# Gate and up products with their last 64 rows paired in the array's rows, column chunks in pairs, a written order on every engine, and the normalization on Pool

## The chip, the cores and the metric

The kernel runs on one core of a Trainium2 chip. The metric is device time in microseconds (us), the median over runs. A core has five engines that run at the same time and wait for each other through semaphores: TensorE (PE; its weight loads are listed as PEld), VectorE (DVE), ScalarE (ACT), GpSimd (Pool) and SyncE (SP), which here only issues transfers. Transfers run on 16 DMA engines; SP and Pool each have a queue into them. SBUF is the working memory of 128 partitions, PSUM the memory into which TensorE accumulates; here it is used as eight banks of 128 x 512 float32.

## The reference, cut to what matters

```python
x  = A_x                                  # [1, 2048, 576]
xn = _layernorm(x)                        # mean and variance over 576, eps 1e-5
s  = attention(xn, wq, k_cache, v_cache, wo)     # 32 heads, head width 128
gate = xn @ w_gate                        # [2048, 4608]
up   = xn @ w_up                          # [2048, 4608]
h    = sigmoid(gate) * up
g    = silu(h @ w_down)                   # [2048, 576]
out  = x + s * g
# returned: out and its gradients for x, k_cache, v_cache, wq, wo, w_gate, w_up, w_down
```

The first stage computes layernorm and the two products with `w_gate` and `w_up` (Wg, Wu). For the backward pass it keeps, beside `h`, the two factors `a = sigmoid(gate)` and `b = h * (1 - a)`.

## The kernel before, in words

The 2048 rows of x are 16 tiles of 128 rows (`st`). The width 576 is four slices of 128 and a last one of 64 (`dts`, `DT` = 5). The width 4608 is nine column chunks of 512 (`FCH`, `NFC`).

**Stage 1** (lines 164 to 263) is all that the change rewrites.

- *Loads.* SP loads two x tiles (L183), then chunk 0 of Wg and Wu, slice by slice (L194, L195), then the other 14 x tiles (L197), then chunks 1 and 2, then 3 to 5 and 6 to 8. The last slice has 64 rows; the other 64 partitions of `wg_sb`, `wu_sb` and `xnT` are set to zero by Pool (`zpad`, L160), so that every product runs over 128 rows.
- *Normalization*, `ln_tile` (from L207): statistics on DVE (L211, L213), square root on ACT (L215), reciprocal and bias on DVE (L216, L219), the scaling on ACT (L220). Then `transpose_to` turns the tile with five TensorE transposes (L59) and copies them to `xnT` on DVE (L42) and ACT (L40).
- *Products.* Three groups of three chunks; within a group all 16 row tiles; within a tile the three chunks. Each chunk takes five products into `g_ps` (L249) and five into `u_ps` (L252), 128 x 128 by 128 x 512, one PSUM bank each. Tiles are normalized two ahead during the first group.
- *After the products*, per chunk: two sigmoids on ACT (L253 gives `a`, L255 gives 1 - a as `oma`), `h` and `b` on DVE (L256, L257). Per tile and group Pool issues one store each to the arrays `h_d`, `a_d`, `b_d` (L259, L262, L263), 384 KB each.
- Pool also issues the store of the normalized x (L235) and the load of Wd (L236).
- The order on every engine is chosen by the scheduler of the language from priorities and dependencies.

**Stage 2** (from L265) reads `h` back transposed (`hT`, two loads issued in stage 1 at L261 and the others by `load_hT` at L282; the first two lie in the room that x had, the others in the room of the weights), multiplies by Wd (L306: per row tile 36 steps of one 512-wide and one 64-wide product) and forms the gradients of the silu.

**The rest**: 32 attention heads forward and backward in an order written out by hand on TensorE, DVE and ACT, then the output product, the gradients of the weights (which read `a`, `b`, `h` in `load_abh`; L806 and L812 are the gradient of Wg and Wu, L779 the product that precedes it) and the gradient of x. In L812 the last 64 columns of x are multiplied twice into the two halves of the output partitions, so two half-width products stand side by side in the array's columns.

Of the kernel before, what the change touches and what calls it, by code (L numbers as in the profile page):

```python
# [9 lines left out]
bf = mybir.dt.bfloat16  # L10
f32 = mybir.dt.float32
# [84 lines left out]
def kernel(  # L96
# [42 lines left out]
    a_d = dram.tile([S, F], bf, name="a_d")  # L139
    b_d = dram.tile([S, F], bf, name="b_d")  # L140
    h_d = dram.tile([S, F], bf, name="h_d")
# [9 lines left out]
    eps_t = pers.tile([P, 1], f32, name="eps_t")  # L151
    nc.vector.memset(eps_t[:], EPS)

    alt = Alt(nc)
    KPAD = dts[-1][1] < P
    d_last, kd_last = dts[-1]

    def zpad(t):
        if KPAD:
            nc.gpsimd.memset(t[kd_last:, DT - 1, :], 0.0)  # L160

    def kfull(i, kd):
        return P if KPAD else kd

    FCH = min(512, F)
    NFC = F // FCH
    GRP = ldiv(NFC, 3)
# [6 lines left out]
    zpad(xnT)  # L174
    dsT = pk.tile([P, DL, S], bf, name="dsT")
    wo_h = pk.tile([P, D], bf, name="wo_h")
    with tc.tile_pool(name="pa", bufs=1) as pa:
        wd_sb = pa.tile([P, FT, D], bf, name="wd_sb")
        with tc.tile_pool(name="a1w", bufs=1) as wp:
            a0x = tc.alloc_tile_pool(name="a0x", bufs=1, side="right")  # L180
            x_all = a0x.tile([P, NT, D], bf, name="x_all")
            XF = min(2, NT)
            nc.sync.dma_start(x_all[:, 0:XF, :], x2[0:XF * P, :].rearrange("(t p) d -> p t d", p=P))  # L183
            xn_st = x_all
            wg_sb = wp.tile([P, DT, F], bf, name="wg_sb")
            wu_sb = wp.tile([P, DT, F], bf, name="wu_sb")
            zpad(wg_sb)
            zpad(wu_sb)
            WSPL = GRP * FCH
            bounds = [0, FCH] + list(range(WSPL, F + 1, WSPL)) if WSPL > FCH else list(range(0, F + 1, WSPL))  # L190
            for bi in range(len(bounds) - 1):
                c0, c1 = bounds[bi], bounds[bi + 1]
                for i, (d0, kd) in enumerate(dts):
                    nc.sync.dma_start(wg_sb[:kd, i, c0:c1], B_w_gate[d0:d0 + kd, c0:c1])  # L194
                    nc.sync.dma_start(wu_sb[:kd, i, c0:c1], B_w_up[d0:d0 + kd, c0:c1])  # L195
                if bi == 0 and NT > XF:
                    nc.sync.dma_start(x_all[:, XF:, :], x2[XF * P:, :].rearrange("(t p) d -> p t d", p=P))  # L197
            FMAX = nc.vector.BN_STATS_FMAX
            nchunk = 1
            while D % nchunk != 0 or D // nchunk > FMAX:  # L200
                nchunk += 1
            with tc.tile_pool(name="a0", bufs=3) as sb0, tc.tile_pool(name="a0ps", bufs=2, space=PSUM) as ps0, \
                    tc.tile_pool(name="a1r", bufs=2) as rows, tc.tile_pool(name="a1t", bufs=3) as tmpp, \
                    tc.tile_pool(name="a1ps", bufs=3, space=PSUM) as ps:

                def ln_tile(st):
                    xt = x_all[:, st, :]  # L207
                    stats = sb0.tile([P, nchunk, nc.vector.BN_STATS_DIM], f32, name="stats")
                    xr = xt.rearrange("p (c f) -> p c f", c=nchunk)
                    for c in range(nchunk):  # L210
                        nc.vector.bn_stats(stats[:, c, :], xr[:, c, :])  # L211
                    mv = sb0.tile([P, nc.vector.BN_AGGR_DIM], f32, name="mv")
                    nc.vector.bn_aggr(mv[:], stats[:])  # L213
                    std = sb0.tile([P, 1], f32, name="std")
                    nc.scalar.activation(std[:], mv[:, 1:2], AF.Sqrt, bias=eps_t[:], scale=1.0)  # L215
                    nc.vector.reciprocal(rstd_all[:, st:st + 1], std[:])  # L216
                    xn_t = xn_st[:, st, :]
                    nbias = sb0.tile([P, 1], f32, name="nbias")
                    nc.vector.scalar_tensor_tensor(nbias[:], mv[:, 0:1], -1.0, rstd_all[:, st:st + 1], op0=ALU.mult, op1=ALU.mult)  # L219
                    nc.scalar.activation(xn_t, xt, AF.Identity, bias=nbias[:], scale=rstd_all[:, st:st + 1])  # L220
                    transpose_to(nc, ps0, xn_t, D, xnT, st * P, ident, alt)

                LA = 2
                for st in range(min(LA, NT)):
                    ln_tile(st)
                for grp in range(NFC // GRP):
                    if grp == 1:
# [3 lines left out]
                    for st in range(NT):  # L231
                        if grp == 0 and st + LA < NT:
                            ln_tile(st + LA)
                        if grp == 0 and st == NT - 1:
                            nc.gpsimd.dma_start(xn_d[:, :].rearrange("(t p) d -> p t d", p=P), xn_st[:])  # L235
                            nc.gpsimd.dma_start(wd_sb[:], B_w_down.rearrange("(t p) d -> p t d", p=P))  # L236
                        srows = slice(st * P, (st + 1) * P)
                        a_row = rows.tile([P, GRP * FCH], bf, name="a_row")
                        b_row = rows.tile([P, GRP * FCH], bf, name="b_row")
                        h_row = rows.tile([P, GRP * FCH], bf, name="h_row")  # L240
                        for c in range(GRP):
                            fc = grp * GRP + c
                            fs = slice(fc * FCH, (fc + 1) * FCH)
                            cs = slice(c * FCH, (c + 1) * FCH)
                            g_ps = ps.tile([P, FCH], f32, name="g_ps")
                            u_ps = ps.tile([P, FCH], f32, name="u_ps")
                            for i, (d0, kd) in enumerate(dts):
                                kk = kfull(i, kd)
                                nc.tensor.matmul(g_ps[:], lhsT=xnT[:kk, i, srows], rhs=wg_sb[:kk, i, fs], start=(i == 0), stop=(i == DT - 1))  # L249
                            for i, (d0, kd) in enumerate(dts):  # L250
                                kk = kfull(i, kd)
                                nc.tensor.matmul(u_ps[:], lhsT=xnT[:kk, i, srows], rhs=wu_sb[:kk, i, fs], start=(i == 0), stop=(i == DT - 1))  # L252
                            nc.scalar.activation(a_row[:, cs], g_ps[:], AF.Sigmoid)  # L253
                            oma = tmpp.tile([P, FCH], bf, name="oma")
                            nc.scalar.activation(oma[:], g_ps[:], AF.Sigmoid, scale=-1.0)  # L255
                            nc.vector.tensor_tensor(h_row[:, cs], u_ps[:], a_row[:, cs], op=ALU.mult)  # L256
                            nc.vector.tensor_tensor(b_row[:, cs], h_row[:, cs], oma[:], op=ALU.mult)  # L257
# [724 lines left out]
```

## Time and profile before

| | us |
|---|---|
| three runs | 5168.2, 5173.1, 5188.1 |
| median | 5173.1 |
| the profiled execution | 5171.4 |
| its span, first to last instruction | 5169.6 |
| mean granted clock of TensorE | 0.994 of full speed |
| first product of stage 1 | 8.24 |
| first product of stage 2 | 350.0 |
| first product of the attention stage (L424) | about 500 |

Times in the profile are counted from the span's start. A group line gives the source line, the engine, the operation, what it writes and reads, the shape, the count, then busy time and the mean of one in ns, then the idle time of the engine just before it and what ended that. A chain of waits is followed back from the last instruction, at each step to what released it.

### The profile page before, as it was taken

What the parts mean: (1) busy time and instruction counts of PE and PEld (TensorE: products, weight loads), DVE (VectorE), ACT (ScalarE), POOL (GpSimd) and SP (SyncE); (2) the same over time, 40 slices, a digit from 0 to 9 for tenths busy, and PEclk for the clock granted to TensorE, in tenths of its full rate; (3) what the DMA queues carried; (4) which work ended last, traced back from release to release, by engine and by line L of the source; (5) the groups of instructions that cost most, each with busy time, mean ns of one, the idle gap of its engine ahead of it and who ended that gap; (6) DMA issues with size and microseconds to landing.
All of it is one profiled execution on the core that took longest, in us unless ns stands there. A gap on an engine that the chain in (4) does not pass through costs nothing.

```text
span 5169.6 us, 125543 instructions
## 1 busy us (share of the span) xinstructions
PE 5042.8 (98%) x54160; PEld 3506.0 (68%) x54160; DVE 3245.6 (63%) x5063; ACT 2288.2 (44%) x2886; POOL 1389.8 (27%) x1978
## 2 busy tenths in 40 slices
PE   8999999999999999999999999999989999999999
PEld 3444777777777777777777777777755666554554
DVE  5545888888888888888888888888733222210111
ACT  6531665565566555655655665566501222100000
POOL 2222332233233323332332333233222222111000
PEclk9999999999999999999999999999999999999999
DMA  7486999999999999999999999999998776697775
GB/s 280 183 215 162 194 193 200 190 195 198 193 197 194 193 191 197 199 199 196 200 194 196 199 193 200 199 198 198 207 223 230 203 202 191 194 249 164 159 152 119
DMA packets 2710366, 1013.31 MB, mean 196 GB/s; under 512 B 2523312, under 2 KB 2643888, under 8 KB 2709808
## 3 DMA queue, kind: packets, MB, share of 16 engines
q1 hardware_dynamic: 2628256, 726.57, 81.3%
q0 software_dynamic: 81552, 278.70, 18.0%
q8 instruction: 423, 6.93, 0.5%
q14 instruction: 135, 1.11, 0.1%
HBM read 172.54 MB, written 201.00 MB: 72 GB/s over the span
## 4 chain that ended last, share of the span: by engine, by line
PE 85%; DVE 6%; DMA 5%; issue 3%; ACT 0%; SPq 0%; POOL 0%; DVEq 0%; ACTq 0%; POOLq 0%
PE acckv L544 15%; PE acc L525 14%; PE acc L923 8%; PE dp L495 8%; PE sp L465 6%; PE accw L806 5%; DVE sneg L467 5%; PE accp L424 4%; PE dh L779 3%; PE g_ps L249 3%; PE u_ps L252 3%; PE acc L306 3%; PE accd L793 3%; DMA dST<-dSq 3%; PE acc L861 2%
## 5 line engine op out<-in xcount | busy, mean ns | idle before, releaser
L476 ACT ACTIVATE Pq<-sneg,nm 128x2048 bf16<-128x2048 bf16 x512 | 1024.5, 2001 | 389.5 <-DVE sneg L467 386.4
L525 PE MATMUL acc<-Kn,dST 128*128 128x128 bf16 x8192 | 1065.2, 219 | 34.6 <-DMA dST<-dSq 34.0
L525 PE MATMUL acc<-Vn,PT 128*128 128x128 bf16 x8192 | 1025.2, 219 | 10.5 <-DMA PT<-Pq 10.3
L544 PE MATMUL acckv<-dOn,Pq 128*128 128x128 bf16 x8192 | 1034.5, 219 | 0.0
L498 DVE SCALAR_TENSOR_TENSOR dSq<-dp,delta,Pq 128x1024 bf16<-128x1024 f32 x608 | 773.4, 1280 | 355.7 <-PE dp L495 353.3
L544 PE MATMUL acckv<-Qn,dSq 128*128 128x128 bf16 x8192 | 894.9, 219 | 0.0
L525 PEld LDWEIGHTS <-dST 128*128 128x128 bf16 x8192 | 757.8, 98 | 172.2 <-DMA dST<-dSq 44.7
L544 PEld LDWEIGHTS <-Pq 128*128 128x128 bf16 x8192 | 794.7, 98 | 117.2 <-issue 0.9
L525 PEld LDWEIGHTS <-PT 128*128 128x128 bf16 x8192 | 767.2, 98 | 153.8 <-DMA PT<-Pq 14.5
L544 PEld LDWEIGHTS <-dSq 128*128 128x128 bf16 x8192 | 718.0, 98 | 99.6
L467 DVE TENSOR_SCALAR_CACHE_REDUCE sneg<-sp,nm 128x1024 bf16<-128x1024 f32 x512 | 656.4, 1282 | 83.7 <-PE sp L465 57.8
L467 DVE TENSOR_SCALAR_CACHE_REDUCE sneg<-sp 128x1024 bf16<-128x1024 f32 x512 | 625.0, 1221 | 59.7 <-PE sp L465 51.5
L501 ACT ACTIVATE t<-dp,negdelta 128x1024 bf16<-128x1024 f32 x416 | 464.1, 1116 | 423.6 <-PE dp L495 354.9
L465 PE MATMUL sp<-KT,QT 128*128 128x512 bf16 x2048 | 609.0, 379 | 34.4 <-DVE sneg L467 27.5
L495 PE MATMUL dp<-VT,dOT 128*128 128x512 bf16 x2048 | 609.5, 379 | 0.7 <-DVE dSq L498 0.7
L484 POOL TENSOR_TENSOR dOn<-dOn,rinv_all 128x256 bf16<-128x256 bf16 x256 | 156.3, 610 | 656.4 <-DVE rinv_all L480 539.5
L505 DVE TENSOR_TENSOR dSq<-t,Pq 128x1024 bf16<-128x1024 bf16 x416 | 319.9, 769 | 0.0
L806 PE MATMUL accw<-dd_blk,xn_all 128*128 128x512 bf16 x1152 | 251.6, 379 | 0.0
L936 DVE SCALAR_TENSOR_TENSOR junk<-dxn,xn_all 128x576 f32<-128x576 f32 x16 | 12.1, 758 | 368.7 <-ACT dxn L931 368.7
L923 PEld LDWEIGHTS <-cf 128*128 128x128 bf16 x2304 | 146.2, 98 | 142.9 <-DMA cf<-dg_d 4.1
L591 POOL DMA_DIRECT2D dq_d<-dq_n x128 | 98.9, 773 | 481.8 <-DVE dq_n L590 473.4
L806 PEld LDWEIGHTS <-xn_all 128*128 128x128 bf16 x1152 | 111.5, 98 | 133.8
(179 smaller groups left out, 6760.2 us busy)
## 6 DMA issues: line engine op xcount, KB each, us to landing
out_dram<-kv POOLq DMA_DIRECT2D x256, 128.0 KB, 5.0
h_d<-h_row POOLq DMA_DIRECT2D x48, 384.0 KB, 2.7
a_d<-a_row POOLq DMA_DIRECT2D x48, 384.0 KB, 2.6
b_d<-b_row POOLq DMA_DIRECT2D x48, 384.0 KB, 3.2
a_blk<-a_d SPq DMA_DIRECT2D x18, 1024.0 KB, 5.7
b_blk<-b_d SPq DMA_DIRECT2D x18, 1024.0 KB, 20.8
du_d<-dd_blk POOLq DMA_DIRECT2D x18, 1024.0 KB, 8.3
dg_d<-dd_blk POOLq DMA_DIRECT2D x18, 1024.0 KB, 11.6
```

Of the source, the lines that this page charges most:

```text
L424: nc.tensor.matmul(acc[:], lhsT=w[:, i, :], rhs=srcT[:, i, cs], start=(i == 0), stop=False)
L465: nc.tensor.matmul(sp[:, c * CH:(c + 1) * CH], lhsT=hs.QT[:, qs], rhs=hs.KT[:, hf * HW_ + c * CH: hf * HW_ + (c + 1) * CH], start=True, st ...
L467: nc.vector.tensor_scalar(sneg[:, hf * HW_:(hf + 1) * HW_], sp[:], -SCALE, None if hf == 0 else nm[:, hf - 1:hf], op0=ALU.mult, op1=ALU.mi ...
L476: nc.scalar.activation(Pq[:], sneg[:], AF.Exp, bias=nm[:, hf:hf + 1], scale=-1.0, accum_out=hs.rs_all[:, qt:qt + 1])
L495: nc.tensor.matmul(dp[:, c * CH:(c + 1) * CH], lhsT=hs.dOT[:, qs], rhs=hs.VT[:, hf * HW_ + c * CH: hf * HW_ + (c + 1) * CH], start=True, s ...
L498: nc.vector.scalar_tensor_tensor(dSq[:, hsl], dp[:], hs.delta[:, qt:qt + 1], Pq[:, hsl], op0=ALU.subtract, op1=ALU.mult)
L501: nc.scalar.activation(t[:], dp[:], AF.Identity, bias=hs.negdelta[:, qt:qt + 1], scale=1.0)
L505: nc.vector.tensor_tensor(dSq[:, hsl], t[:], Pq[:, hsl], op=ALU.mult)
L525: nc.tensor.matmul(bx.acc[:, j, :], lhsT=T[qt][:, kt, :], rhs=getattr(hs, rhs)[:, kt, :], start=(kt == 0), stop=(kt == NT - 1))
L544: nc.tensor.matmul(bx.acc[i][:, jj, :], lhsT=slabs[qt][:, k0:k0 + P], rhs=getattr(hs, rhs)[:, qt, :], start=(qt == 0 and jj == 0), stop=(q ...
L806: nc.tensor.matmul(acc[:], lhsT=xn_all[:, st, i * P:(i + 1) * P], rhs=dd_blk[:, st, :, :], start=(st == 0), stop=(st == NT - 1))
L923: nc.tensor.matmul(accs[sl][j][:, :nn], lhsT=ch[:, kk, sl * P:(sl + 1) * P], rhs=w_[:, n0:n0 + nn], start=(pi == 0 and kk == 0), stop=(las ...
```

## The change

- One array `abh_d` [3, 2048, 4608] replaces `a_d`, `b_d` and `h_d`; its readers are adapted.
- x tiles get 640 columns: the last 64 columns of the normalized tile are copied once more behind it, so that the fifth transpose gives the same 64 rows in both halves of the partitions. The zero padding goes. A new tile `wl_sb` holds the last 64 rows of Wg in partitions 0 to 63 and of Wu in 64 to 127.
- Four products of 128 rows per accumulation stay (`main`). The fifth has 64 rows (`fifth`): Wg's uses the upper half of the array's rows, Wu's the lower, into different PSUM banks, one issued right after the other.
- Work goes in *units* of two accumulations of Wg and two of Wu (four PSUM banks): a row tile with a pair of chunks, for the ninth chunk two row tiles. Two units, A and B, form one iteration: A's full products, A's fifths, B's fifths (which open B's accumulation), B's full products. So the eight half-height products of A and B stand together.
- ACT and DVE work on 1024 columns at a time. Per unit Pool issues one store of a, b and h (two in the last group).
- Normalization: variance plus eps on DVE, its power -1/2 on Pool, and the scaling in one step, on DVE for the first four tiles and on Pool for the other twelve. The copies to `xnT` are all on ACT. No square root runs on ACT.
- All five engines follow the written order in this stage. SP: x tile 0, x tile 1, chunk 0, chunk 1, x tiles 2 and 3, x tiles 4 to 15, the other chunks in pairs, Wd, then the first two loads of `hT`, which are issued in the last chunk's group instead of the last third. In the first group (16 tiles, chunks 0 and 1) tiles n+4 and n+5 are normalized and turned in iteration n, between B's products and B's sigmoids.
- One product loop of a later stage (L779) drops a helper that had no effect there.

The core of the diff, new lines only:

```python
def load_wgu(c0, c1):
    cs = slice(c0 * FCH, c1 * FCH)
    for k, (w, src) in enumerate(((wg_sb, B_w_gate), (wu_sb, B_w_up))):
        nc.sync.dma_start(w[:, :, cs], src[:DL * P, cs].rearrange("(t p) c -> p t c", p=P))
    for k, src in enumerate((B_w_gate, B_w_up)):
        nc.sync.dma_start(wl_sb[k * KL:(k + 1) * KL, cs], src[DL * P:, cs])

def ln(st, norm):
...
    nc.vector.bn_aggr(mv[:], stats[:])
    nc.vector.tensor_scalar(vpe[:], mv[:, 1:2], EPS, None, op0=ALU.add)
    nc.gpsimd.tensor_tensor(rstd_all[:, st:st + 1], vpe[:], mhalf[:], op=ALU.pow)
    norm.tensor_scalar(xt[:, :D], xt[:, :D], mv[:, 0:1], rstd_all[:, st:st + 1], op0=ALU.subtract, op1=ALU.mult)
    norm.tensor_copy(xt[:, D:], xt[:, DL * P:D])

def transpose_x(st):
    pt = ps.tile([P, 2, 8, P], bf, name="pt", tag="b")
    for k in range(2):
        for i in range(DT):
            nc.tensor.transpose(pt[:, k, i, :], x_all[:, st + k, i * P:(i + 1) * P], ident[:])
    for k in range(2):
        nc.scalar.copy(xnT[:, :, (st + k) * P:(st + k + 1) * P], pt[:, k, :DT, :])

def main(un, first, js=(0, 1)):
    for j in js:
        st, c = un.jobs[j]
        for acc, w in ((un.g, wg_sb), (un.u, wu_sb)):
            for i in range(DL):
                nc.tensor.matmul(acc[:, j, :], lhsT=xnT[:, i, st * P:(st + 1) * P], rhs=w[:, i, c * FCH:(c + 1) * FCH],
                                 start=(first and i == 0), stop=(not first and i == DL - 1))

def fifth(un, first, js=(0, 1)):
    for j in js:
        st, c = un.jobs[j]
        for k, acc in enumerate((un.g, un.u)):
            r = slice(k * KL, (k + 1) * KL)
            nc.tensor.matmul(acc[:, j, :], lhsT=xnT[r, DL, st * P:(st + 1) * P], rhs=wl_sb[r, c * FCH:(c + 1) * FCH],
                             start=first, stop=not first)

def out(un):
    r_ = rows.tile([P, 3, 2, FCH], bf, name="abh")
    nc.scalar.activation(r_[:, 0, :, :], un.g[:], AF.Sigmoid)
    oma = tmpp.tile([P, 2, FCH], bf, name="oma")
    nc.scalar.activation(oma[:], un.g[:], AF.Sigmoid, scale=-1.0)
    nc.vector.tensor_tensor(r_[:, 2, :, :], un.u[:], r_[:, 0, :, :], op=ALU.mult)
    nc.vector.tensor_tensor(r_[:, 1, :, :], r_[:, 2, :, :], oma[:], op=ALU.mult)
    return r_
...
for n in range(0, len(units), 2):
    A, B = Unit(units[n]), Unit(units[n + 1])
...
        main(A, True)
        fifth(A, False)
        fifth(B, True)
        ra = out(A)
        main(B, False)
    if gi == 0:
        for st in (n + 4, n + 5):
            if st < NT:
                ln(st, nc.gpsimd)
        if n + 4 < NT:
            transpose_x(n + 4)
    rb = out(B)
    store(A, ra)
    store(B, rb)
```

More of the change, by code (lines that the diff above doesn't have):

```diff
@@ L180 @@
             a0x = tc.alloc_tile_pool(name="a0x", bufs=1, side="right")
[L181 to L206, printed above, removed]
+            x_all = a0x.tile([P, NT, DT * P], bf, name="x_all")
@@ L220, in ln_tile @@
[L220 to L227, printed above, removed]
+                    vpe = sb0.tile([P, 1], f32, name="vpe")
+                    nc.vector.tensor_scalar(vpe[:], mv[:, 1:2], EPS, None, op0=ALU.add)
```

132 lines of the change are left out of this document (71 added, 61 removed).

## The prediction

> **What bounds the kernel now.** I read the page first: busy shares, clock, and the chain that ended last.
>
> ```profile
> PE 5042.8 (98%) x54160; PEld 3506.0 (68%) x54160; DVE 3245.6 (63%) x5063; ACT 2288.2 (44%) x2886; POOL 1389.8 (27%) x1978
> PE 85%; DVE 6%; DMA 5%; issue 3%; ACT 0%; SPq 0%; POOL 0%; DVEq 0%; ACTq 0%; POOLq 0%
> ```
>
> TensorE is the bound, and the changed lines L249 and L252 hold only 3% of the chain each. So I read that stage by itself. Its end, from the timeline of TensorE (start, length, then what ran):
>
> ```profile
> 48.30 1.06 PE L59 MATMUL pt<-ident,x_all 128*128 128x128 bf16 x10
> 52.42 2.08 PE L249 MATMUL g_ps<-wg_sb,xnT 128*128 128x512 bf16 x5 [3.06 <-ACT oma L255]
> 54.30 2.13 PE L252 MATMUL u_ps<-wu_sb,xnT 128*128 128x512 bf16 x5
> 56.26 1.24 PE L249 MATMUL g_ps<-wg_sb,xnT 128*128 128x512 bf16 x5
> ...
> 348.93 1.24 PE L252 MATMUL u_ps<-wu_sb,xnT 128*128 128x512 bf16 x5
> 350.00 2.34 PE L306 MATMUL acc<-wd_sb,hT 128*128 128x512 bf16 x17
> ```
>
> The stage hands over at 350.0 us with no gap. Five products take 1.079 us there (347.85 to 348.93), 0.2158 each, so its 1440 take 310.8. Its 80 transposes take about 0.1 each (ten in the 1.06 above): 8.0. The remaining 31.2 us are a late start, waits and a slow clock, all before 60 us:
>
> ```profile
> 8.00:12.00 4.00, 4.00 (x11) 1.45 (x11) 0.42 (x1) 1.80 (x3) 4.00 (x2) 1.00 1.01 338
> 20.00:24.00 4.00, 1.37 (x4) 0.36 (x3) 2.90 (x8) 1.72 (x3) 0.00 (x0) 0.50 1.04 364
> 44.00:48.00 4.00, 4.00 (x20) 1.85 (x19) 3.89 (x22) 3.74 (x10) 0.72 (x2) 1.00 1.02 410
> ```
>
> Columns: stretch, its length, busy time of PE, PEld, DVE, ACT, POOL, granted clock, DMA share, GB/s. From 20 to 24 us TensorE works a third of the time at half clock while the DMA engines are full: the waits of TensorE there name the weight loads (6.6 and 3.8 us), and the load of Wd, which this stage does not need, shares the engines. From 60 us on TensorE waits for nothing here.
>
> **The change, part by part** (times after, counted from the span's start to the hand-over).
>
> Products: four full ones per accumulation stay, 1152 x 0.2158 = 248.6. The 288 half-height ones should run as 144 pairs. No row here shows two products side by side in the array's rows; the nearest are two side by side in its columns (timeline of TensorE):
>
> ```profile
> 3943.50 0.38 PE L806 MATMUL accw<-dd_blk,xn_all 128*128 128x512 bf16 x1
> 3943.81 0.41 PE L812 MATMUL accw<-dd_blk,xn_all 128*64 128x256 bf16 x4
> ...
> 3945.68 8.91 PE L779 MATMUL dh<-wdT,doBT 128*128 128x256 bf16 x80
> ```
>
> And from the chain that ended last, in order of time:
>
> ```profile
> 3943.88 1.87 PE accw L812 x32
> 3945.75 8.84 PE dh L779 x80
> ```
>
> Thirty-two half-width products take 1.87 us, 0.058 each, where a full-width one of the same length takes 8.84/80 = 0.1105: a pair costs one. So 144 x 0.2158 = 31.1; at the other end, no overlap, 62.2. I take the first, the row it is nearest to. The Trainium skill, "TensorE: Matmul & The Clock Gate", Part 3 (measured speedup), gives four row tiles 3.07 times, 77% of four; at that share the pairs would take 40.4, an estimate, and the sum below 9.3 more. No run here shows row tiles.
>
> Entering and leaving: from the last L806 (3943.50) to the first L779 (3945.68) are 2.18 us; one product (0.216) and 16 pairs at 0.1105 make 1.98, so two changes of form cost 0.20. Gathering makes one entry and exit per two units, 36 in all: 7.2 (bounds 0 and 11.7, the latter 72 x 0.163, the 0.379 of a product less its step).
>
> Start. The two first x tiles and two chunks of both weights (2.65 MB after the first 0.30 MB) now stand before x tiles 2 and 3, and TensorE's written order puts the transposes of tiles 2 and 3 before the first product. The first x tiles land at 3.64 us (statistics L211 start then). At 353 GB/s (8 to 30 us) the rest takes 7.5, so 11.1; at the 272 GB/s by which 3.54 MB had landed at 15.57, 13.4. I take 11.5. Two normalizations follow on DVE: statistics 2 x 0.44, aggregate 0.20, add 0.15, the power on Pool with hops 0.35, normalize at most 0.58 (L946), copy 0.1: 2.3 each, then 0.5 of transposes: first product at 16.5 (15 to 19), where it was 8.24. It then runs without weight waits, since Wd moves behind all weights on SP and what it shared the engines with is gone. A cold first window: ten products above took 4.2 us instead of 2.16, so 2. The other 60 transposes: 6.0.
>
> Waits in the first column group. In six of its eight iterations ten transposes stand between main B and the next main A, and TensorE waits there for Pool. The rows:
>
> ```profile
> L501 ACT ACTIVATE t<-dp,negdelta 128x1024 bf16<-128x1024 f32 x416 | 464.1, 1116 | 423.6 <-PE dp L495 354.9 <-DVE delta L578 26.2 <-issue 21.1
> L505 DVE TENSOR_TENSOR dSq<-t,Pq 128x1024 bf16<-128x1024 bf16 x416 | 319.9, 769 | 0.0
> L580 POOL TENSOR_TENSOR o_n<-ou,rinv_all 128x512 bf16<-128x512 bf16 x128 | 133.3, 1042 | 0.2 <-DMA on_d<-o_n 0.2
> L320 POOL CAST g2b<-g 128x1152 bf16<-128x1152 f32 x8 | 13.8, 1724 | 65.8 <-DVE g L312 65.6
> L579 POOL TENSOR_SCALAR negdelta<-delta 128x4 f32<-128x4 f32 x128 | 27.8, 217 | 258.4 <-DVE delta L578 258.4
> L452 POOL TENSOR_SCALAR rsc<-rinv_all 128x16 f32<-128x16 f32 x32 | 8.4, 262 | 2.7
> ```
>
> Count from the last extra pair of A. TensorE still has B's two pairs, the exit and 16 products: free at T = 4.2. ACT's first sigmoid (1.116) ends at 1.54; DVE's h (1.28, as L498 at this width) at 2.9, b (0.769) at 3.8; only then, by the written order, the statistics of tile n+4 (2 x 0.4, 0.2, 0.15) at T+0.7 and of n+5 at T+1.75. Pool per tile: power about 0.22 (L579), normalize 576 wide between 0.86 (L320's rate) and 1.17 (L580's), by the slope of L579 to L452 (3.75 ns an element) 2.4; copy 0.2 (the memset L404 of 64x128 takes 0.201); in all p = 1.45, bounds 1.2 and 2.85. So Pool is through at T+0.7+2p = T+3.6, the last transposes at T+4.2, of which 1.0 is their own: 3.2 waited, 19.2 for six. ACT's two copies (0.7 each) and then B's sigmoids are queued behind them; the next fifth of B needs those PSUM buffers 4 us later, and they are free 0.4 before. Had ACT been 1 us slower, that would be the next wait.
>
> Clock in these gaps: the window of 3.06 us idle above was followed by half clock, and the new gaps (1.5, then 0.9) are shorter; the window from 3677.63 was 46% busy and was followed by half clock too. I take 2 us, bounds 0 and 12. The Trainium skill, same page, "Why this matters for your kernels", warns of gaps over about 3 us; by that rule it is 0, and the sum 2 less. The 3.06 us row agrees, the 46% row does not.
>
> Hand-over: Wd's first accumulation takes the PSUM of the last B, which its sigmoids free 2.4 us after the last product (L501's 1.116 twice, overlapped by 0.1, and the matmul's tail); 2.4, where it was 0.
>
> At nothing: wider ACT and DVE steps (ACT 4.5, DVE 4.1 of an 8.0 us iteration; uncovered, they would be longer than nothing only past 8). Pool's 80 store issues for 144, half a us each, lie under TensorE; three row buffers give each store some 8 us to land, and issues landed in 2.6 to 3.2 at half the size. The two first loads of transposed h are issued about 21 us before the hand-over instead of 90; they held SP's queue 6.2 and 11.4 us, so they end about 3 us early. That cover gone costs at most 15.
>
> Sum: 16.5 + 2 + 248.6 + 31.1 + 7.2 + 6.0 + 19.2 + 2 + 2.4 = 335.0, against 350.0: -15. Every later instruction keeps its order on every engine. The profiled execution took 5171.4 (span 5169.6), 1.7 under the median of 5173.1; I subtract from the median: 5158.
>
> **The rivals.**
> 1. The gaps close. p = 1.2 (-3), free form changes (-7), no cold clock (-4), no hand-over wait (-2.4): -31, 5142. For: each end is a bound above. Against: b before the statistics is written order.
> 2. Pool decides, and it is slower than before. The sum is -15 + 12 x (p - 1.45): even at p = 2.7. A power costing 2 us, which no row shows, makes p = 3.2, +21 in six iterations, +4 in the first four tiles: +10, 5183. For: the slope of the small Pool rows. Against: L580, L320.
> 3. The half-height products do not share the array: +31, that is +16, 5189. It is also the case in which the change doesn't do what it says; the page's 77% lies between. Against: the L812 pairs.
> 4. Transposed h is late: up to +15, 5173.
>
> **Chances.** Forecast 0.47 (its own range 5146 to 5170), rival 1 0.24, rival 2 0.14, rival 3 0.10, rival 4 0.05. About 0.5%, 26 us, is what a measurement of this kernel can tell from no change. Faster by more: most of rival 1 (0.20) and a tail of the forecast (0.06), 0.26. Slower by more: tails of rivals 2 (0.03), 3 (0.04) and 4 (0.02), 0.09. Same 0.65. The range 5134 to 5190 reaches from past rival 1 to rival 3.
>
> **What would show it.** First Wd product near 335 us. Pairs of extra products starting together, their pairs 0.216 apart, and 0.1 more at each change of form. First product near 16.5, preceded by a wait for x. In the first group six waits of TensorE for Pool's copy or normalize, together near 19 us; Pool's tile near 1.45. No wait later but one near 2.4 for ACT at the hand-over. Wrong if Pool's normalize is far from 1 us, the extra products step singly, or stores hold up ACT.

## The result, and the profile after

| | before | after |
|---|---|---|
| median, timed together (first chip) | 5172.4 | 5212.7 |
| ratio, first timing | | 1.0074, interval 1.0049 to 1.0099 |
| ratio, second timing, another chip | | 1.0048, interval 1.0030 to 1.0067 |
| span of the first profiled execution | 5169.6 | 5204.8 |
| first Wd product | 350.0 | 368.6 |
| Wd's stage | 150.5 | 154.3 |
| attention stage | 3280.4 | 3292.6 |
| the rest | 1388.8 | 1389.3 |

All in us but the ratios. The kernel is slower, by some 25 to 38 us, where 5158 and "no change" had been forecast. In the first pair of profiles the spans differ by 35.2: 18.6 up to the first Wd product, 3.8 in Wd's stage, 12.2 in the attention stage (first query projection to first output projection), 0.5 behind it.

From the page of after, busy shares and the chain that ended last:

```profile
PE 4982.3 (96%) x53232; PEld 3492.4 (67%) x54160; DVE 3221.2 (62%) x4895; ACT 2243.8 (43%) x2696; POOL 1396.5 (27%) x1950
PE 82%; DMA 7%; DVE 6%; issue 4%; POOL 1%; ACT 0%; SPq 0%; DVEq 0%; ACTq 0%; POOLq 0%
```

TensorE still bounds the whole, but its share of the chain fell from 85% to 82%. (Some matmul records are missing here, 53232 of 54160, so its busy time is not compared.) What it waits for in stage 1 is in the view of waits of after, 0 to 372 us (total, times, longest):

```profile
PE pt L204 <- POOL x_all L197: 37.8, 12, 5.1
PE pt L204 <- DVE x_all L197: 16.4, 4, 7.5
PE acc L345 <- ACT oma L234: 3.2, 1, 3.2
PE g_ps L227 <- ACT oma L234: 1.4, 1, 1.4
```

The first line is the largest, twice the 19.2 us that the forecast gave it. The second is the start: x tile 2, which the forecast had landed at 11.5 us, was there at 13.7, as VectorE's first statistics of it show in the timeline of after.

```profile
13.71 0.82 DVE L191 BATCH_NORM_STATS2 stats<-x_all 128x6 f32<-128x288 bf16 x2 [5.69 <-DMA x_all<-in_A_x_dram]
```

One iteration of the first group shows both what went right and what went wrong, in the timeline of TensorE of after:

```profile
42.80 0.39 PE L227 MATMUL g_ps<-wl_sb,xnT 64*128 64x512 bf16 x1
42.80 0.39 PE L227 MATMUL u_ps<-wl_sb,xnT 64*128 64x512 bf16 x1
43.02 0.38 PE L227 MATMUL g_ps<-wl_sb,xnT 64*128 64x512 bf16 x1
43.02 0.38 PE L227 MATMUL u_ps<-wl_sb,xnT 64*128 64x512 bf16 x1
...
43.77 1.04 PE L219 MATMUL g_ps<-wg_sb,xnT 128*128 128x512 bf16 x4
...
46.37 1.03 PE L219 MATMUL u_ps<-wu_sb,xnT 128*128 128x512 bf16 x4
50.78 0.71 PE L204 MATMUL pt<-ident,x_all 128*128 128x128 bf16 x5 [3.39 <-POOL x_all L197]
53.99 0.72 PE L204 MATMUL pt<-ident,x_all 128*128 128x128 bf16 x5 [2.50 <-POOL x_all L197]
54.50 1.91 PE L219 MATMUL g_ps<-wg_sb,xnT 128*128 128x512 bf16 x4
56.21 1.63 PE L219 MATMUL u_ps<-wu_sb,xnT 128*128 128x512 bf16 x4
57.68 1.03 PE L219 MATMUL g_ps<-wg_sb,xnT 128*128 128x512 bf16 x4
```

The half-height products start two at a time, 0.22 apart, the time of one full product. Then TensorE stands before the transposes of the next two tiles, once for each, and the eight products behind the gap take 3.18 us (54.50 to 57.68) in place of 8 x 0.2158 = 1.73. Pool's groups of after, 0 to 130 us, give the price of a tile:

```profile
L197 POOL TENSOR_SCALAR x_all<-x_all,mv,rstd_all 128x576 bf16<-128x576 bf16 x12 | 27.5, 2291 | 1.3
L196 POOL TENSOR_TENSOR rstd_all<-vpe,mhalf 128x1 f32<-128x1 f32 x16 | 8.9, 558 | 49.3 <-DVE vpe L195 35.9 <-DMA wl_sb<-in_B_w_up_dram 13.4
L198 POOL COPY x_all<-x_all 128x64 bf16<-128x64 bf16 x12 | 2.8, 237 | 0.8
```

A tile takes 2.29 + 0.56 + 0.24 and 0.1 between them, 3.2 us from the start of one power to the next. By windows (columns as before):

```profile
62.00:79.00 17.00, 10.93 (x51) 4.67 (x51) 6.10 (x13) 5.15 (x7) 7.75 (x8) 0.80 0.36 139
130.00:160.00 30.00, 29.84 (x149) 12.74 (x152) 14.53 (x16) 13.64 (x15) 6.50 (x8) 1.00 0.72 268
```

In the first group TensorE works 10.9 of 17 us at a granted clock of 0.80; from 130 us on it works without a gap at full clock, and an iteration takes 7.98 us, 29 times in a row. The six long ones take 16.35 to 17.05, together 101.1 (101.3, 101.3 and 104.2 in three later profiles of the same kernel). Last, the end of the stage in the same timeline:

```profile
359.24 0.38 PE L227 MATMUL u_ps<-wl_sb,xnT 64*128 64x512 bf16 x1
360.97 0.37 PE L227 MATMUL g_ps<-wl_sb,xnT 64*128 64x512 bf16 x1 [1.35 <-ACT oma L234]
...
364.44 1.03 PE L219 MATMUL u_ps<-wu_sb,xnT 128*128 128x512 bf16 x4
368.64 3.70 PE L345 MATMUL acc<-wd_sb,hT 128*128 128x512 bf16 x17 [3.18 <-ACT oma L234]
```

and what ScalarE itself waited for there, 330 to 372 us of after:

```profile
ACT abh L232 <- DMA abh_d<-abh: 9.2, 3, 5.4
```

ScalarE, which had to free the PSUM, was itself held by a store that had not left its row buffer: the last group's stores (384 KB) took 9.9 us at the median to land, where the groups before took 3.9 for 768 KB. From the issues of after, 300 to 372 us (size, median to landing):

```profile
abh_d<-abh POOLq DMA_DIRECT2D x9, 768.0 KB, 3.9
abh_d<-abh POOLq DMA_DIRECT2D x16, 384.0 KB, 9.9
```

The three later profiles have 6.6, 6.6 and 8.3 us for the second line. The first two loads of transposed h stand in the same engines (SP's queue, 342.3 to 357.9).

### The profile page after: what moved, and what is told of

It reads as the page before. It is cut to its first block, busy times and chain, and to the rows that moved or that the text cites. A ratio compares the mean times of both kernels' runs of the same rounds, so it can differ in the third digit from the quotient of the medians.

```text
span 5204.8 us, 124030 instructions
## 1 busy us (share of the span) xinstructions
PE 4982.3 (96%) x53232; PEld 3492.4 (67%) x54160; DVE 3221.2 (62%) x4895; ACT 2243.8 (43%) x2696; POOL 1396.5 (27%) x1950
## 4 chain that ended last, share of the span: by engine, by line
PE 82%; DMA 7%; DVE 6%; issue 4%; POOL 1%; ACT 0%; SPq 0%; DVEq 0%; ACTq 0%; POOLq 0%
PE acckv L583 16%; PE acc L564 14%; PE acc L961 8%; PE dp L534 6%; PE sp L504 5%; DVE sneg L506 5%; PE accw L844 4%; PE accp L463 4%; DMA dST<-dSq 4%; PE dh L817 3%; PE accd L831 3%; PE acc L899 2%; PE acc L762 2%; PE acc L345 2%; PE g_ps L219 2%
## 5 line engine op out<-in xcount | busy, mean ns | idle before, releaser
L564 PE MATMUL acc<-Kn,dST 128*128 128x128 bf16 x8192 | 1068.0, 219 | 39.2 <-DMA dST<-dSq 36.7
L564 PE MATMUL acc<-Vn,PT 128*128 128x128 bf16 x8192 | 1025.0, 219 | 14.2 <-DMA PT<-Pq 12.2
L504 PE MATMUL sp<-KT,QT 128*128 128x512 bf16 x1763 | 548.4, 380 | 32.6 <-DVE sneg L506 25.8
L534 PE MATMUL dp<-VT,dOT 128*128 128x512 bf16 x1728 | 541.4, 380 | 0.8 <-DVE dSq L537 0.8
L219 PEld LDWEIGHTS <-xnT 128*128 128x128 bf16 x1152 | 112.8, 101 | 149.5 <-issue 30.0
## 6 DMA issues: line engine op xcount, KB each, us to landing
dg_d<-dd_blk POOLq DMA_DIRECT2D x18, 1024.0 KB, 11.4
```

What stands on the lines that cost most here:

```text
L219: nc.tensor.matmul(acc[:, j, :], lhsT=xnT[:, i, st * P:(st + 1) * P], rhs=w[:, i, c * FCH:(c + 1) * FCH], start=(first and i == 0), stop=( ...
L504: nc.tensor.matmul(sp[:, c * CH:(c + 1) * CH], lhsT=hs.QT[:, qs], rhs=hs.KT[:, hf * HW_ + c * CH: hf * HW_ + (c + 1) * CH], start=True, st ...
L534: nc.tensor.matmul(dp[:, c * CH:(c + 1) * CH], lhsT=hs.dOT[:, qs], rhs=hs.VT[:, hf * HW_ + c * CH: hf * HW_ + (c + 1) * CH], start=True, s ...
L564: nc.tensor.matmul(bx.acc[:, j, :], lhsT=T[qt][:, kt, :], rhs=getattr(hs, rhs)[:, kt, :], start=(kt == 0), stop=(kt == NT - 1))
```

## The experiments

All change the kernel after, unless something else is said. "Iteration" is the distance of the first half-height products of two iterations; there are eight iterations in the first group, and the six with a Pool tile in them are the long ones.

### Who is waited for in the first group

Normalization back on VectorE for all tiles:

```diff
-                                    ln(st, nc.gpsimd)
+                                    ln(st, nc.vector)
```

> The scaling and the copy of the 64 columns run on VectorE for all sixteen tiles, as they already do for the first four; all else as in the changed kernel. Theory P (TensorE waits in the written order for the normalization, and Pool's 3.2 us a tile sets the wait): VectorE takes 2.47 us a tile in the first four, so the last transposes of an iteration come 2.2 us sooner, six times 2 to 3 us: the six long iterations of 16.4 to 17.1 us become about 14.3, the kernel 12 to 18 us faster, near 5197. Rival C (the cold clock after each gap is the larger part): gaps under 5 us no longer cool the clock and the gain is over 25 us. Rival N (Pool is not what TensorE waits for): no change.

Measured: ratio to before 0.9995 (0.9976 to 1.0015), iterations 14.56 falling to 13.69, first Wd product at 346.4 instead of 368.6. The same operation on VectorE, from its groups, 0 to 130 us:

```profile
L197 DVE TENSOR_SCALAR x_all<-x_all,mv,rstd_all 128x576 bf16<-128x576 bf16 x16 | 6.9, 429 | 10.8 <-POOL rstd_all L196 10.8
```

429 ns against 2291. TensorE's waits in the six iterations fall from 37.8 to 22.4 us, the iterations together from 101.1 to 83.8: 17.3 of the 27.7 us by which they missed the forecast (waits 18.6, clock 9.1). The 22.4 us are left because a tile's normalization still starts only behind the same iteration's h and b. Theory P had the iterations nearly right (14.3). The first Wd product gains 22.3 us, more than its 12 to 18; the other 5 lie at the start and the end of the stage, which the edit does not touch. Rival C's condition fails, and with it the idea that short gaps keep the clock. From the second of the six iterations on the gaps are now 1.46 and 2.01 us, and the products behind them still run slowly, in TensorE's timeline of this run:

```profile
45.24 0.45 PE L204 MATMUL pt<-ident,x_all 128*128 128x128 bf16 x5 [1.46 <-DVE x_all L197]
47.71 0.55 PE L204 MATMUL pt<-ident,x_all 128*128 128x128 bf16 x5 [2.01 <-DVE x_all L197]
48.05 1.91 PE L219 MATMUL g_ps<-wg_sb,xnT 128*128 128x512 bf16 x4
49.75 1.82 PE L219 MATMUL u_ps<-wu_sb,xnT 128*128 128x512 bf16 x4
51.41 1.03 PE L219 MATMUL g_ps<-wg_sb,xnT 128*128 128x512 bf16 x4
```

Eight products take 3.36 us here (48.05 to 51.41), in place of 1.73. Over the six iterations they lose 8.2 us, against 9.2 in after.

The same work one step earlier, still on Pool:

```diff
-            with tc.tile_pool(name="a0", bufs=4) as sb0, tc.tile_pool(name="a1r", bufs=3) as rows, \
+            with tc.tile_pool(name="a0", bufs=8) as sb0, tc.tile_pool(name="a1r", bufs=3) as rows, \
...
+                for st in range(4, 6):
+                    ln(st, nc.gpsimd)
...
-                            for st in (n + 4, n + 5):
+                            for st in (n + 6, n + 7):
```

> Pool still normalizes, but tiles n+6 and n+7 in iteration n instead of n+4 and n+5, tiles 4 and 5 ahead of the loop, and the small statistics tiles get eight buffers instead of four; TensorE still turns n+4 and n+5 in iteration n. Theory P: the waits of TensorE on Pool in the first group go, the six iterations fall from 17 to about 9 us, Wd's first product moves from 368.6 to about 322, the kernel to about 5166. Rival S (Pool is the bound of the first group: two tiles of 3.2 us and two stores of 0.8 are 8.1 of a 9 us iteration, and stores issued late hold up ScalarE): the iterations fall to 11 to 13 only, and the kernel stays over 5180.

Measured: ratio 0.9963 (0.9947 to 0.9980), first Wd product at 326.9; iterations 7.48, 9.21, 17.16, 9.21, 9.21, 9.21. TensorE's waits of this kernel, 0 to 330 us, no longer name Pool:

```profile
PE pt L204 <- DVE x_all L197: 16.2, 4, 7.2
PE g_ps L227 <- ACT oma L234: 4.6, 1, 4.6
PE u_ps L219 <- ACT xnT L206: 3.1, 6, 0.5
```

So Pool is fast enough (6.5 us for two tiles in an iteration of 9.2) and only asked too late. The clock, too, is granted in full from 64 to 100 us, which puts the cold products down to the gaps. The one long iteration left is the second line (0.81 of the clock from 46 to 64 us): ScalarE waited 6.0 us for a store while SP's loads of the later weights filled the DMA engines. Its waits, 0 to 330 us:

```profile
ACT abh L232 <- DMA abh_d<-abh: 17.3, 8, 6.0
```

That is the sign rival S gave for late stores, once; its iterations of 11 to 13 us did not come.

### The start

x tiles 2 and 3 loaded ahead of the weights:

```diff
                 load_x(1, 2)
+                load_x(2, 4)
                 load_wgu(0, 1)
                 load_wgu(1, 2)
-                load_x(2, 4)
```

> The load of x tiles 2 and 3 stands before the weights of chunks 0 and 1 on SP; all else as in the changed kernel. Theory P with its late start: VectorE normalizes the four first tiles without a gap, 2.47 us each from 3 us on, and the first product comes at about 13.3 instead of 19.1: 5 to 6 us faster, near 5207. Rival W (the weights of chunk 0 land that much later, and the start is bound by them): no change within 2 us.

Measured: first product at 13.2 instead of 19.1, ratio 1.0037 (1.0016 to 1.0057). The six iterations took 17.9 falling to 17.1 (together 104.1), which is not enough to take the gain back; the fourth profile of after has the same (104.2) without this edit, so the edit need not be their cause. The first Wd product came at 361.7, and the start is bound by x tiles 2 and 3, not by the weights of rival W.

### The end of the stage

Three arrays and three stores for a unit, as before the change (the readers follow):

```diff
-    abh_d = dram.tile([3, S, F], bf, name="abh_d")
+    a_d = dram.tile([S, F], bf, name="a_d")
+    b_d = dram.tile([S, F], bf, name="b_d")
+    h_d = dram.tile([S, F], bf, name="h_d")
...
+                    for k, d_ in ((2, h_d), (0, a_d), (1, b_d)):
+                        if s0 == s1:
+                            nc.gpsimd.dma_start(d_[s0 * P:(s0 + 1) * P, c0 * FCH:(c1 + 1) * FCH], r_[:, k, :, :].rearrange("p j c -> p (j c)"))
```

> Three arrays for a, b and h as in the kernel before, and three stores of a third each per unit; all else as in the changed kernel. In the profiled runs the time from Wd's first product on is 4819.6 before and 4836.2 after; 5 of these 17 us lie in the Wd stage, 11 in the attention heads. Theory M (the joined array or its large stores cost time later): that stretch goes back to about 4820 and the kernel to about 5196. Theory J (the heads vary from run to run by 10 us or more for reasons of transfer timing): the stretch may come out anywhere from 4815 to 4845, and in the other runs of this call too.

Measured: ratio 1.0055 (1.0030 to 1.0080), first Wd product at 377.0, attention stage 3292.1 us. The end was worse with smaller stores, not better: ScalarE waited 14.5 us for stores of b there, and TensorE 6.9 us for it. Separate arrays shorten neither Wd's stage (158.7) nor attention.

The single chunk's group made second instead of last:

```diff
             groups = [[c for c in (c0, c0 + 1) if c < NFC] for c0 in range(0, NFC, 2)]
+            groups.insert(1, groups.pop())
```

> The group with the one remaining column chunk is made second instead of last, nothing else. Theory L: the first h loads are issued some 50 us ahead of the end of stage 1 and not 23; the waits of ScalarE for stores at the end (12 us) and the hand-over (3.2 us) go, so that the first Wd product comes at 352 to 360 us instead of 368.6, and the stage of Wd falls from 154 to 162 us to 150.5 within 2. Whole: 5184 to 5200 on this measure, 12 to 22 us under the changed kernel. Rival L0 (the stores are too large for the transfers wherever that group stands, and the slow h landings come of the other layout): the 12 us of store waits come back in the second group, where the Wd weights are being loaded too, and the Wd stage stays at 154 or more; no gain over 5 us.

Measured: ratio 1.0031 (1.0007 to 1.0054), first Wd product at 366.6, Wd's stage 151.7. ScalarE no longer waits for stores at the end, and the 384 KB stores land in 3.6 us at the median in their new place, so rival L0 falls. The loads of transposed h now leave earlier; SP's queue in this kernel's timeline:

```profile
313.04 15.40 SPq L303 DMA_TRANSPOSE hT<-abh_d  x2
```

The cause is right and its price was set too high: theory L asked for the first Wd product at 352 to 360 us. The first group took 2.7 us more than in after (17.7 to 17.1), which lies in that kernel's own scatter, and up to the first query projection 4.6 us are gained against the first profile of after (518.3 for 522.9), 7.6 against the mean of four. So small a gain is what L0 allowed too (5 us); it falls by the landing times and by Wd's stage.

### The two terms that the forecast had right

Both half-height products of a pair in the same rows:

```diff
-                            r = slice(k * KL, (k + 1) * KL)
+                            r = slice(0, KL)
```

> Both half-height products of a pair use the lower 64 rows of the array, so that they can't lie side by side; the second one multiplies by Wg's last 64 rows in place of Wu's, so up's last 64 terms are wrong. Theory A (two products in disjoint rows run at the same time, each pair costing one product): the steady iterations grow from 7.98 to 8.84 us (four pairs, 0.2158 us each), the first Wd product comes some 27 to 31 us later than 368 to 371, and the two products of a pair start 0.21 us apart. Rival (they only share the weight load or the hand-over, and the array works them off one by one): 7.98 stays.

Measured: iterations 8.84 instead of 7.98, first Wd product 396.3. The timeline of TensorE of this kernel:

```profile
227.27 0.39 PE L227 MATMUL g_ps<-wl_sb,xnT 64*128 64x512 bf16 x1
227.50 0.38 PE L227 MATMUL u_ps<-wl_sb,xnT 64*128 64x512 bf16 x1
227.72 0.38 PE L227 MATMUL g_ps<-wl_sb,xnT 64*128 64x512 bf16 x1
227.93 0.38 PE L227 MATMUL u_ps<-wl_sb,xnT 64*128 64x512 bf16 x1
```

Now they step singly, 0.215 to 0.23 apart. The pairing is worth 0.86 us in each iteration that does not wait, all that it could be. The six long iterations hide it, though: they take 17.9 falling to 17.1 without it and as much with it in the fourth profile of after. So the first Wd product moves by 27.7 us against the first profile of after (27.4 against the mean of four), not by 36 x 0.86 = 31.

The half-height products not gathered over two units:

```diff
                             fifth(A, False)
-                            fifth(B, True)
                             ra = out(A)
-                            main(B, False)
+                            main(B, True)
+                            fifth(B, False)
```

> The half-height products of the second unit of an iteration go behind its full ones instead of beside the first unit's: two stretches of half-height products in each iteration, not one. Theory F (each change of form costs 0.095 us, in and out): steady iterations 8.17 us in place of 7.98, first Wd product 5 to 7 us later. Forecast's own figure, 0.2 us for both changes together, gives the same; rival (the order costs nothing): 7.98.

Measured: 4.10 and 4.10 instead of 7.98, that is 8.20 for two units: 0.22 us for one more stretch of half-height products, 8 us over the stage. The first Wd product at 373.1 comes 4.5 us later than in the first profile of after; the long iterations hide a part here too.

### The attention stage: scatter or not

The instructions from Wd's stage on are the same and in the same order, yet the first profiles differ by 12.2 us in attention. Further profiles of both kernels, and a closer timing:

> The kernel before once more, for a second profile. Theory J (the length of the attention stage differs from execution to execution by 5 to 20 us, whatever stands ahead of it): the stretch from the first query projection to the first output projection differs from the first profile's 3280.4 us by more than 3 us. Rival C (the changed stage 1 lengthens it by what it leaves behind): it repeats 3280.4 within 3 us. Both: the stage of Wd, whose h loads are issued some 90 us ahead of their use, repeats 150.5 us within 1.5, and its first product comes at 349.8 within 2.

> The changed kernel once more, for a second profile. Both theories: first product 18 to 20 us, six long iterations of 16.3 to 17.1 us, first Wd product at 368.6 within 3 us. Theory L (the h loads that lost their lead cost the Wd stage time each time): Wd stage 154 to 162 us again, the longest h landing over 24 us. Rival: it was one execution's accident, and the stage is back at 150.5 within 1.5. Theory J on the attention stage: it differs from 3292.6 us by more than 3 us; rival C: it repeats that.

> The changed kernel against the kernel before once more, timed closely. Up to the first query projection the two profiles of each kernel give 522.9 and 525.2 us against 500.5 and 512.2, a difference of 17.7 us. Theory J (what the attention stage shows beside that differs from execution to execution and belongs to neither kernel): ratio 1.0034, within 0.0025. Rival C (the attention stage is 19 us longer for the change, by the means of 3268.0 in two profiles before and 3291.8 in eight profiles of changed kernels, less the spread): ratio 1.0065 to 1.008.

> The kernel before, a third profile. Theory J (attention's length scatters from execution to execution alike in both kernels): of three further profiles before, at least one has an attention stage of 3285 us or more, and their mean with the first two (3280.4 and 3264.7) is 3280 or more. Rival C (the changed kernels' stage is longer by 15 to 20 us): all three at 3264 to 3281, mean under 3276. For the first 500 us: first query projection at 500 to 512 us.

> The kernel before, a fourth profile, as the third: theory J 3270 to 3295 us for the attention stage, rival C 3264 to 3281.

> The kernel before, a fifth profile, as the third: theory J 3270 to 3295 us for the attention stage, rival C 3264 to 3281.

> The changed kernel, a fourth profile, on the same chip as the three before: both theories 3283 to 3300 us for the attention stage and a first query projection at 522 to 528 us.

| profile | first Wd product | Wd's stage | attention | rest | span |
|---|---|---|---|---|---|
| before, first | 350.0 | 150.5 | 3280.4 | 1388.8 | 5169.6 |
| before, four more | 361.5, 361.7, 356.4, 356.8 | 150.7 each | 3264.7, 3275.0, 3284.4, 3279.0 | 1399.6, 1406.4, 1400.6, 1390.5 | 5176.5, 5193.8, 5192.2, 5177.0 |
| after, first | 368.6 | 154.3 | 3292.6 | 1389.3 | 5204.8 |
| after, three more | 371.2, 366.1, 369.6 | 154.1, 161.9, 157.8 | 3296.1, 3298.6, 3293.1 | 1390.0, 1389.4, 1391.4 | 5211.4, 5216.0, 5211.8 |
| difference of the means | +11.6 | +6.4 | +18.4 | -7.2 | +29.2 |

The ratio of after_timed, 1.0048, is 24.9 us on 5190.3. Neither theory holds as put. The three further profiles before have no attention stage of 3285 or more, and their mean with the first two is 3276.7, between what J (3280 or more) and C (under 3276) asked for; the timed ratio lies within J's interval and under C's. But no attention stage of after is as short as the longest one before, and the stage behind it is 7 us shorter: in three of the five profiles before TensorE waits 5.7 to 8.7 us in the output product for loads of its input oT, in none of after. Attention and the rest together take 4664.3 to 4685.1 us before and 4681.9 to 4688.0 after, so the two kernels overlap there. The attention stage's wait is for the transposing load of dS, in five profiles before 22.0 to 37.6 us, mean 31.1, in four of after 36.7 to 46.5, mean 42.2. One of each, from the waits of TensorE in that stage, the third profile before and then the fourth of after:

```profile
PE acc L525 <- DMA dST<-dSq: 27.5, 23, 9.0
```

```profile
PE acc L564 <- DMA dST<-dSq: 46.5, 38, 9.4
```

That is 11 of the 18 us. Why the same loads, in the same order, are late more often, no run tells. One profile with separate arrays (3292.1) speaks against the layout in DRAM. The eight other variants have 3283.0 to 3299.8, four of them within 2 us of the longest stage before (3284.4), so even that the change lengthens this stage is likely and not shown. It stays open.

Two things of the kernel before show up as well: its first profile, from which the forecast was made, was the best of five in stage 1, by 7.3 us against their mean, and in the others TensorE waits longer for the weights' loads. The waits of the third profile before, 0 to 375 us:

```profile
PE g_ps L249 <- DMA wg_sb<-in_B_w_gate_dram: 10.9, 4, 7.2
```

(6.6 in the first). And Wd's stage is 150.5 to 150.7 in every profile before, 154.1 to 161.9 in every one of after, with waits for transposed h of 1.8 to 8.8 us: this is the change.

### The causes together

The tiles one step earlier, x tiles 2 and 3 first and the single chunk's group second, each as above, and Wd loaded from Pool's queue in the third group:

```diff
-                        nc.sync.dma_start(wd_sb[:], B_w_down.rearrange("(t p) d -> p t d", p=P))
...
+                        if gi == 2 and n == 0:
+                            nc.gpsimd.dma_start(wd_sb[:], B_w_down.rearrange("(t p) d -> p t d", p=P))
```

> Four edits together: normalization one step further ahead on Pool, the x blocks loaded ahead of the weights, the single chunk's group second, and the Wd weights loaded from Pool's queue in the third group. If the three causes found so far (six waits on Pool, 47 us; the start, 6 us; stores and h loads at the end, 12 to 20 us) are the whole difference and add: first product 13.2 us, iterations 9.2 in the first group with none over 11, last product near 311, first Wd product near 312, Wd stage 150.5, and a span of 5130 to 5160 us; ratio to before 0.992 to 0.996. Rival N (the first group is then bound by the weights' transfers, which the earlier x blocks delay): one or two iterations of 14 to 18 us stay, first Wd product at 322 to 330, ratio 0.995 to 0.999.

Measured: ratio 0.9920 (0.9897 to 0.9944), span 5159.2; first product 13.3, first Wd product 330.7, Wd's stage 150.7, two long iterations (16.2 and 18.4). The ratio is the one expected if the causes add; the two long iterations are what rival N expected. Then the same with the loads in pieces:

```diff
-                for g in groups[1:]:
-                    load_wgu(g[0], g[-1] + 1)
+                paced = {(0, 6): 8, (0, 10): 2, (0, 12): 3, (1, 0): 4, (1, 2): 5, (1, 4): 6, (1, 6): 7}
...
+                        if (gi, n) in paced:
+                            c = paced[gi, n]
+                            load_wgu(c, c + 1, nc.gpsimd)
+                        if gi == 2 and n < 12:
+                            wt = slice(n * FT // 12, (n + 2) * FT // 12)
+                            nc.gpsimd.dma_start(wd_sb[:, wt, :], B_w_down[wt.start * P:wt.stop * P, :].rearrange("(t p) d -> p t d", p=P))
```

> As the four edits together, but the weights behind the first pair of chunks and the Wd weights are loaded chunk by chunk from Pool's queue, one piece in an iteration. If the two long iterations that were left (16.2 and 18.4 us) come of stores that wait behind 9 and 5 MB of loads issued at once: no iteration over 10 us, last product at 311 to 313, first Wd product at 312 to 314, Wd stage 150.7, and 15 to 19 us under the four edits: ratio to before 0.988 to 0.990. Rival (the store's wait has another cause, such as the packets of the first iterations' own stores): one of the long iterations stays, ratio 0.990 to 0.992.

Measured: ratio 0.9919 (0.9890 to 0.9948), span 5148.1; no iteration over 10.1, first Wd product at 320.5. The long iterations did come of loads issued in bulk, but only 10 us of the 17 expected came back, and the ratio is the rival's (0.990 to 0.992). ScalarE's waits for stores in this kernel, 0 to 330 us:

```profile
ACT abh L233 <- DMA abh_d<-abh: 49.0, 18, 5.6
```

They are many and small, and cost TensorE 3.5 us directly. By the timing the two versions can't be told apart; both are faster than the kernel before and than the change.

## Why the prediction was wrong

| term of the forecast | forecast | measured | off by |
|---|---|---|---|
| start, first product | 16.5 | 19.1 | +2.6 |
| cold first window | 2 | 2 | 0 |
| an iteration of products, pairs and form changes | 7.97 | 7.98 | +0.4 in all |
| transposes in the six long iterations | 6.0 | 6.0 (not separated) | 0 |
| waits for Pool in them | 19.2 | 37.8 | +18.6 |
| slow clock behind them | 2 | 11.1 (what is left) | +9.1 |
| stores at the end | 0 | 1.9 | +1.9 |
| hand-over | 2.4 | 3.3 | +0.9 |

Together 33.5 of the 33.6 us by which the first Wd product missed 335.0. The six long iterations take 101.1; with the eight products (1.7) that the first iteration has ahead they are 54.9 us above six of 7.98. Of these, 37.8 are the waits, 6.0 the transposes, and 11.1 is left: 9.2 in the eight products behind the gaps of the six, the other 1.9 not traced. The start's 2.6 is the late landing of x tile 2 (13.7 for 11.5) and two tiles of 2.47 us on VectorE where 2.3 was taken.

**The step that failed is Pool's price, p = 1.45.** The path was right, TensorE waiting for Pool in six iterations, and the forecast's formula for them with the measured 3.23 gives +21 on them, close to the +18.6. The forecast had the right row before it: the slope of the two small TENSOR_SCALAR rows, L579 and L452, gave 2.4 us: the same operation on the same engine at other widths. It measured 2.29. I set it aside for two rows of other operations (a cast, a two-tensor product) that were nearer in width. Here the same operation was the better guide. The power, priced 0.22 by a small TENSOR_SCALAR, took 0.56. Rival 2 had the mechanism, and only a seventh of the chance. Its p of 3.2 was near by luck: it came from a power of 2 us, where the scaling took most of the time. The Trainium skill, "GPSIMD Engine Reference", section 3.1, puts an element on Pool at some 2.6 cycles against one on VectorE. The trace does not agree for this operation: it has 2291 against 429 ns for the same instruction, 5.3 times.

**The clock** was the second miss, and it did not hang on Pool's price: I took 2 us of bounds 0 to 12, on the ground that the gaps would be short (1.5 and 0.9 us). With Pool's price the gaps were 3.39 and 2.50 us with 0.7 of transposes between them, and the products behind ran at about half pace, in all six. With VectorE's price they were 1.46 and 2.01 in five of the six (3.16 and 1.91 in the first), near the forecast's, and the products lost 8.2 us all the same. In that run TensorE was 13 to 20% busy in the 3.41 us before the clock fell (44.51 to 47.92, and the same in the two iterations behind it). So of the two rows that the forecast weighed, the window that was 46% busy was the better guide, not the single gap of 3.06 us. The Trainium skill, "TensorE: Matmul & The Clock Gate", section "Why this matters for your kernels", warns of gaps over some 3 us; the trace does not bear that out as a limit here, since the gaps of 1.46 and 2.01 us stayed under it and were followed by slow products. Two gaps and the little work between them acted together.

**"At nothing"** failed at the end of the stage. The stores were held against those of the stretch before, with 8 us to land; in the last group each carried half as much in 512-column pieces, landed in 9.9 us, and the two loads of transposed h stood in the same engines. Of the 15 us that rival 4 set for the lost lead of the loads of transposed h, Wd's stage took 3.6 to 11.4 in the four profiles.

**"Every later instruction keeps its order"** was right and did not carry what was built on it: with the same order, attention took 18 us more by the means, and the rest 7 less.

**What held**: the pairs (rival 3 falls), the form changes (0.20 forecast; 0.31 less 0.22 on entering and again on leaving, 0.19), the steady iteration to 0.01 us, and no wait later in the stage. From pair to pair it took 0.215 to 0.227 us, as from one full product to the next. The Trainium skill, "TensorE: Matmul & The Clock Gate", section "Measured speedup vs the span model", has 3.07 times for four row tiles, the 77% of the forecast; two row tiles lose nothing here. The same section of the Trainium skill gives a span model, one product's duration and some 4 ns for each further tile; the trace agrees, since the two products of a pair start within 10 ns. The cold window's 2 us held although its row was misread: the forecast's ten products take 3.84 us from start to start (52.42 to 56.26), not 4.2, so the row gives 1.7.

## What to carry to other kernels

Price an operation that moves to another engine by a row of that operation on that engine, scaled in width, before a row of the right width and another operation; and where the price is uncertain, ask in the same breath how early its input exists, since one iteration's lead made the slow engine free (ratio 0.9963 to before, against 1.0048 to 1.0074). A wait that came in every iteration was paid twice on TensorE: once as the wait (37.8 us) and once as the slow clock behind it (9 to 11), and gaps of 1.5 and 2 us close together were enough for the second. A second profile of the kernel before costs little and tells how much of a few us in a stage is its own scatter, before a forecast is summed against one execution.

## What the runs showed of the hardware

- Two half-height products in disjoint rows of the array cost one product; two in the same rows cost two (7.98 and 8.84 us an iteration).
- A scaling with two scalars a partition, 128 x 576 in bfloat16, takes 2.29 us on Pool and 0.43 on VectorE; a power of 128 x 1 takes 0.56 on Pool.
- Two gaps of 1.46 and 2.01 us on TensorE with five transposes between them were followed by eight products in 2.84 to 3.36 us, where 1.73 is usual (granted clock 0.88 over an iteration of 14 us).
- A load of 5 MB issued at once (Wd, 19.2 us to land) held up the stores issued behind it in the same queue, and with them ScalarE and TensorE: one iteration of 18.4 us where 7.98 is usual, and none over 10.1 when the loads were issued in pieces.
